# Four second-layer weight blocks converted early and kept in DRAM, and the whole-array block of the scores put first

## The chip, the cores and the metric

The kernel runs on one core of one Trainium2 chip. The metric is the device time of one execution in microseconds (us), the median of the runs shown; lower is better. The engines are TensorE (PE in the profile), VectorE (DVE), ScalarE (ACT), GpSimd (POOL) and SyncE (SP), which issues most DMAs. Each engine works through its own instructions in a fixed order.

## The reference

Three layers follow each other on 4 batches of 448 rows and 768 columns: attention with a sigmoid in place of a softmax, a gated feed-forward (keys, values, receptance), and a Fourier mixing with a second feed-forward.

```python
def _attn_ref(q, k, v):                       # 4 x 12 heads x 448 x 64
    scores = scale * np.matmul(q, k.transpose(0, 1, 3, 2)) - np.log(S)
    attn = 1.0 / (1.0 + np.exp(-scores))
    return np.matmul(attn, v)
def _moe_ref(x, mu_k, mu_r, w_k, w_v, w_r):   # w_k 768 x 1024, w_v 1024 x 768
    x_prev = np.concatenate([zeros, x[:, :-1, :]], axis=1)
    xk = mu_k * x + (1.0 - mu_k) * x_prev
    xr = mu_r * x + (1.0 - mu_r) * x_prev
    k = np.maximum(xk @ w_k, 0.0)
    v = k * k @ w_v
    r = 1.0 / (1.0 + np.exp(-(xr @ w_r)))
    return r * v
def _moe2_ref(x, w_ch1, w_ch2):               # w_ch1 768 x 3072, w_ch2 3072 x 768
    X = np.fft.fft(np.fft.fft(x, axis=1), axis=2)
    u = x + np.real(X)
    un = (u - mean(u)) / np.sqrt(var(u) + 1e-06)
    return u + np.maximum(un @ w_ch1, 0.0) @ w_ch2
```

The weights come as 64-bit floats.

## The kernel before

The program is recorded in an order that a small planner (the class Order, L110) works out: generators such as `attention`, `keys`, `values`, `convert` and `network` yield the time at which they can go on, by costs written into the class, and what they issue is appended to the engines. So a changed cost, wait or task moves instructions of all engines, and at run time each engine keeps to the order that came out.

Products of full precision are made of three matmuls of 448 columns each: every operand is split into a high and a low part (names ending in h and l), and high x high, high x low and low x high are added in PSUM. The stages, in order of time:

**Attention** (0 to about 250 us). The 24 pairs of heads (6 to a batch) go through `scores` and `attnv` (L383, L414). A pair's scores are seven blocks: six of 64 rows, 0 to 5, two of which run side by side in the two halves of the array, and one of 128 rows, block 6 (FULL), that takes the whole array. Their PSUM banks come from `ps2` (five, for the six small blocks) and `ps1` (three, for block 6, the attention output `av` and the tiles `k` of the keys). A sigmoid on ScalarE takes each block out of PSUM (`sg`). Pairs 0 to 5 use plain fp32; from pair 6 on (WHOLE) each block is three split matmuls. Pairs 6 and 7 start with block 6, the later ones end with it (L402). After each pair `join` copies the output out and mixes it with the shifted rows. Between pairs the matmuls of `keys` fill in, as many as the planner puts into PACE (L31) per pair.

**Receptance** (to about 371 us). Meanwhile `load_split` (L256) converts w_v: from the two 32-bit halves of a 64-bit float, bit operations on VectorE and a square on ScalarE make the 32-bit weight, whose low part gets cut off where it is tiny. One block of 128 x 768 is one two-operand and three three-operand instructions of VectorE.

**Values and spectra** (to about 540 us). `values` (L689) multiplies by w_v, VectorE multiplies with the receptance (tiles `rv`, two buffers) into `x2`; per batch `folds`, `spectrum`, `mixed` and `centre` follow on VectorE, ScalarE and TensorE, between the matmuls of the next batch. k tiles are loaded by `load_k2` as their buffers come free.

**The last network**. For batches 0 and 1, `network` (L1133) takes the 12 weight groups one after the other: `ffn1` (w1, tiles `h`), then `ffn2` (w2, tiles `f`, added to `acc` by VectorE, which frees the PSUM bank). Groups 0 and 1 were converted during attention (EARLY, L321) and are loaded. Groups 2 to 11 are converted by `convert` (L976) beside it: load of the 64-bit block, square and bit operations, store into DRAM (`w_d`), high part by ScalarE, low part by GpSimd. `prepare_rows` (L1073) multiplies the rows of batches 2 and 3 by `rsb`. From about 896 us on, batches 2 and 3 go through a scheme of seven products for w1 (`pair1`) and through `ffn2` with the weights from `w_d`. Every second `pair1` begins with a matmul of one column.

Of the kernel before, what the change touches and what calls it, by code (L numbers as in the profile page):

```python
# [12 lines left out]
F32 = mybir.dt.float32  # L13
F32R = mybir.dt.float32r
U32 = mybir.dt.uint32
# [6 lines left out]
D = H * DH  # L22
# [7 lines left out]
TOK = B * S  # L30
PACE = 10.8  # L31
EVERY = (11.6, 9.4)
# [4 lines left out]
PERM = np.concatenate([SL, D - SL, D // 2 - SL, D // 2 + SL, LL, L2])  # L37


TINY = float((2.0**-15 * 1.0625) ** 2)  # L40
# [204 lines left out]
def build(tc, ap):  # L245
# [10 lines left out]
    def load_split(pl, parts, gap=0.0, raws=1, lane=0, eng=None, vector=False, every=0.0):  # L256
# [11 lines left out]
        for i, (wait, src, hi, lo, key) in enumerate(parts):  # L268
# [7 lines left out]
            if callable(hi):  # L276
                hi, lo, after = hi()
            n = o.size(hi)
            if ahead and raws > 1:
                nxt = load(*ahead)  # L280
            if ap["wide"]:
                top, low = raw[:, :, 1], raw[:, :, 0]
                if not vector:
                    w = pl.tile([128, n], F32, tag=f"wst{lane}", name="_".join(map(str, key)), bufs=1)
                bits = pl.tile([128, n], U32, tag=f"wbits{lane}", name="_".join(map(str, (*key, "bits"))), bufs=1)
                if vector:
                    yield o.ts(bits, top, 3, 0x3FFFFFF8, ALU.logical_shift_left, ALU.bitwise_and) - 0.1
                    yield o.stt(bits, top, 0xC0000000, bits, ALU.bitwise_and, ALU.bitwise_or) - 0.1
                    yield o.stt(bits, low, 29, bits, ALU.logical_shift_right, ALU.bitwise_or) - 0.1
                    yield o.tt(V, top.bitcast(F32), top.bitcast(F32), top.bitcast(F32), ALU.mult) - 0.1  # L290
                    w = bits.bitcast(F32)
                    yield o.stt(w, top.bitcast(F32), TINY, w, ALU.is_ge, ALU.mult) - 0.1
                    if ahead and raws == 1:
                        nxt = load(*ahead)
                else:
                    o.act(w, top.bitcast(F32), AF.Square)
                    yield o.ts(bits, top, 3, 0x3FFFFFF8, ALU.logical_shift_left, ALU.bitwise_and) + gap
                    yield o.stt(bits, top, 0xC0000000, bits, ALU.bitwise_and, ALU.bitwise_or) + gap
                    yield o.stt(bits, low, 29, bits, ALU.logical_shift_right, ALU.bitwise_or) + gap
                    if ahead and raws == 1:  # L300
                        nxt = load(*ahead)
                    yield o.stt(w, w, TINY, bits.bitcast(F32), ALU.is_ge, ALU.mult)
            else:
                w = raw
            if vector:
                V.tensor_copy(hi, w)
                o.spend(V, 0.07 + n * 0.00104)
            else:
                yield o.act(hi, w)
# [73 lines left out]
    def scores(i):  # L383
# [16 lines left out]
        else:  # L400
            halves = [(2 * c, 2 * c + 1) for c in range(3)]
            for ns in [(FULL,), *halves] if i < WHOLE + 2 else [*halves, (FULL,)]:  # L402
                ps = {n: room(n) for n in ns}
                for t, (a, b) in enumerate(((0, 0), (0, 1), (1, 0))):
                    for n in ns:
                        c, j = places[n]
                        cost = None if j is None else 0.107
                        o.mm(ps[n][:, 0:S], k[a][rows(j), c], q[b][rows(j)], t == 0, t == 2, cost)
                for n in ns:
                    weigh(i, n, ps[n])  # L410
                yield from o.others()
# [17 lines left out]
    def join(i, ps):  # L429
# [3 lines left out]
        b, p = pairs[i]  # L433
        o.dma(x_d[b][p], x)
        if b > 1:
            yield from o.issued(("key", b - 2))
# [166 lines left out]

    wv_parts = [((), ap["w_v"][:, t], wvh[:, t], wvl[:, t], ("wv", t)) for t in range(NF)]
    NK = 12
    k2_t, un_t, r_t, rs_t = {}, {}, {}, {}
# [42 lines left out]
    o.run(("r_d", B - 1, KD - 1))  # L649
    o.run(("wv", NF - 1))  # L650
    s_r.close()
# [37 lines left out]
    def values():  # L689
        for b in range(B):  # L690
            o.spawn(new_x2(b))
            for e in range(KD):
                while len(o.feed) > 6:
# [243 lines left out]
    w_t = {}  # L937

    def load_early(nm, g, pl):

# [7 lines left out]

    load_early("w1", 0, wq)
    o.spawn(values())  # L950
# [25 lines left out]
    def convert():  # L976
# [19 lines left out]
        for n, (nm, g, i) in enumerate(seq):  # L996
# [12 lines left out]
            w = raw  # L1009
            if ap["wide"]:  # L1010
                top, low = raw[:, :, 1], raw[:, :, 0]
                w = wst.tile([128, D], F32, tag="wst", name=f"{nm}_{g}_{i}", bufs=2)
                bits = wst.tile([128, D], U32, tag="bits", name=f"{nm}_{g}_{i}_bits", bufs=1)
# [332 lines left out]
```

## Time and profile before

| | us |
|---|---|
| three runs | 1231.38, 1226.49, 1226.11 |
| median | 1226.49 |
| profiled execution, its own time | 1231.31 |
| its span, first to last instruction | 1229.5 |
| TensorE busy | 1216.5 (99%) |
| VectorE busy | 907.4 (74%) |
| ScalarE busy | 479.1 (39%) |
| GpSimd busy | 135.3 (11%) |

The busy time of an engine is the time in which at least one of its instructions ran. Matmuls are pipelined: records of neighbours overlap, so the time from one start to the next tells more than a duration. The waits tell whom an engine stood still for. A stretch of time can be asked for each engine's busy time and count of instructions; an instruction that only reaches into the stretch is counted too. All parts of the text that use the word spacing mean the time from one matmul's start to the next one's.

### The profile page before, as it was taken

Reading aid. Unit: us, or ns where it says so; the run is one execution under the profiler, and the core shown is the slowest. Engines: PE = TensorE matmul, PEld = TensorE weight load, DVE = VectorE, ACT = ScalarE, POOL = GpSimd, SP = SyncE. Lnnn points to the kernel's source line nnn. Section 1 sums busy time; section 2 is a strip of 40 time slices with the busy share of each in tenths; the row PEclk is TensorE's granted clock in tenths of the full one; section 3 lists DMA queues with packets and bytes.
Section 4 is the critical chain, followed back from the end, with each engine's and each line's share of the span. In section 5 each row is a group of like instructions: output and inputs, shape, how many; then the busy total and the mean of one; then the engine's idle time right before and its main releaser. Section 6 shows DMA issues by size and latency. Waiting matters only on the chain. (4 is left out here: it accounts for less than half of the span.)

```text
span 1229.5 us, 16416 instructions
## 1 busy us (share of the span) xinstructions
PE 1216.5 (99%) x6142; PEld 1050.5 (85%) x6142; DVE 907.4 (74%) x1425; ACT 479.1 (39%) x864; POOL 135.3 (11%) x97
## 2 busy tenths in 40 slices
PE   8999999999999999999989999999999999999998
PEld 3467766789999998999979999999999999999998
DVE  5776887656853669797999999897566776776654
ACT  5867767766530122142333333332132332322220
POOL 0000000000000000000232232222021111121110
PEclk9999999999999999999999999999999999999999
DMA  6656669666948446396555555555842112121102
GB/s 219 223 169 229 213 239 339 237 243 231 320 158 259 169 165 218 113 316 227 184 202 212 184 200 203 201 186 188 314 141 78 52 54 75 52 66 63 52 1 90
DMA packets 77296, 217.82 MB, mean 177 GB/s; under 512 B 9312, under 2 KB 31776, under 8 KB 76576
## 3 DMA queue, kind: packets, MB, share of 16 engines
q1 hardware_dynamic: 76544, 214.37, 50.3%
q0 software_dynamic: 672, 2.40, 0.6%
q8 instruction: 48, 0.79, 0.3%
q14 instruction: 32, 0.26, 0.1%
HBM read 143.84 MB, written 72.90 MB: 176 GB/s over the span
## 5 line engine op out<-in xcount | busy, mean ns | idle before, releaser
L215 DVE TENSOR_TENSOR acc<-acc,f 128x448 f32<-128x448 f32 x258 | 156.6, 616 | 66.4 <-PE f L180 63.8
L180 PE MATMUL f<-h,w2h 128*128 128x448 f32 x576 | 165.6, 368 | 3.6 <-DVE acc L215 3.6
L180 PE MATMUL f<-un,w1h 128*128 128x448 f32 x576 | 166.2, 368 | 0.0
L180 PE MATMUL f<-h,v2h 128*128 128x448 f32 x576 | 163.6, 365 | 0.0
L180 PEld LDWEIGHTS f<-h,w2h 128*128 128x128 f32 x576 | 107.8, 188 | 14.9 <-DVE acc L215 4.8
L234 ACT ACTIVATE sg<-sc,bias_s 128x448 f32<-128x448 f32 x168 | 95.0, 651 | 60.7 <-PE sc L180 60.7
L180 PEld LDWEIGHTS f<-un,w1h 128*128 128x128 f32 x576 | 108.2, 188 | 10.4 <-issue 0.4
L180 PEld LDWEIGHTS f<-h,v2h 128*128 128x128 f32 x576 | 108.2, 188 | 8.5
L180 PE MATMUL v<-k,wvh 128*128 128x448 f32 x384 | 113.4, 370 | 0.8 <-DMA k<-k_d 0.7
L180 PE MATMUL f<-un,w1l 128*128 128x448 f32 x288 | 105.9, 368 | 0.0
L180 PE MATMUL f<-h,w2l 128*128 128x448 f32 x288 | 105.9, 368 | 0.0
L180 PE MATMUL f<-h,v2l 128*128 128x448 f32 x288 | 105.2, 365 | 0.0
L223 DVE SCALAR_TENSOR_TENSOR w_bits<-w_raw,w_bits 128x768 uint32<-128x768 uint32 x80 | 99.9, 1248 | 1.0
L180 PE MATMUL av<-sg,v 128*64 128x448 f32 (+1 forms) x336 | 81.1, 549 | 0.0
L180 PEld LDWEIGHTS v<-k,wvh 128*128 128x128 f32 x384 | 71.6, 188 | 8.1 <-DMA k<-k_d 2.4
L215 POOL TENSOR_TENSOR v2l<-v,v2h 128x768 fp32r<-128x768 f32 x24 | 46.8, 1970 | 275.0 <-ACT v2h L232 275.0
L215 POOL TENSOR_TENSOR w1l<-w,w1h 128x768 fp32r<-128x768 f32 x20 | 41.2, 2062 | 300.6 <-ACT w1h L232 295.5
L180 PE MATMUL v<-k,wvl 128*128 128x448 f32 x192 | 70.8, 369 | 0.0
L180 PE MATMUL k<-xkh,wkh 128*128 128x448 f32 x192 | 70.7, 368 | 0.0
L180 PE MATMUL k<-xkl,wkh 128*128 128x448 f32 x192 | 70.4, 367 | 0.0
L180 PE MATMUL k<-xkh,wkl 128*128 128x448 f32 x192 | 70.3, 366 | 0.0
L180 PEld LDWEIGHTS av<-sg,v 128*64 128x64 f32 (+1 forms) x336 | 27.9, 144 | 42.5 <-issue 35.9
(175 smaller groups left out, 2356.7 us busy)
## 6 DMA issues: line engine op xcount, KB each, us to landing
w_raw<-in_w SPq DMA_DIRECT2D x40, 768.0 KB, 4.5
w_d<-w SPq DMA_DIRECT2D x40, 384.0 KB, 2.6
k_d<-kp SPq DMA_DIRECT2D x32, 448.0 KB, 2.8
k<-k_d SPq DMA_DIRECT2D x32, 448.0 KB, 6.3
a<-w_d SPq DMA_DIRECT2D x24, 384.0 KB, 3.5
v<-w_d SPq DMA_DIRECT2D x24, 384.0 KB, 3.0
k<-in_k SPq DMA_DIRECT2D x24, 256.0 KB, 5.5
v<-in_v SPq DMA_DIRECT2D x24, 256.0 KB, 3.0
```

The lines of the kernel that those rows point to most:

```text
L180: self.nc.tensor.matmul(out, lhs, rhs, start=start, stop=stop, skip_group_check=skip)
L215: eng.tensor_tensor(out, a, c, op=op)
L223: self.nc.vector.scalar_tensor_tensor(out, a, scalar, c, op0=op0, op1=op1)
L234: self.nc.scalar.activation(out, a, fn, **kw)
```

## The change

Four edits go together.

- AHEAD names groups 2 and 3 of w2, two blocks each. `load_split`, which converts w_v in receptance, gets the two blocks of group 2 at its end and stores them into `w_d`; a new task `ahead` converts those of group 3, in four half blocks, at the beginning of the values, and only then loads w1 of group 0. `convert` loads the four blocks as 32-bit floats from `w_d` and does no bit work on them.
- In `load_split` the square on ScalarE now writes over the raw block, after the second bit operation and not ahead of them, and the separate tile for the weight is gone.
- `scores` starts with block 6 for all pairs from 6 on; `join` waits until the next pair's scores are recorded before it mixes; PACE is 10.6 for 10.8.
- `values` waits until a batch's `x2` tile is taken.

```diff
-PACE = 10.8
+PACE = 10.6
...
+AHEAD = tuple(("w2", g) for g in range(2, 4))
+SOON = 2
...
-                    o.act(w, top.bitcast(F32), AF.Square)
-                    yield o.ts(bits, top, 3, 0x3FFFFFF8, ALU.logical_shift_left, ALU.bitwise_and) + gap
-                    yield o.stt(bits, top, 0xC0000000, bits, ALU.bitwise_and, ALU.bitwise_or) + gap
-                    yield o.stt(bits, low, 29, bits, ALU.logical_shift_right, ALU.bitwise_or) + gap
+                    o.ts(bits, top, 3, 0x3FFFFFF8, ALU.logical_shift_left, ALU.bitwise_and)
+                    yield o.stt(bits, top, 0xC0000000, bits, ALU.bitwise_and, ALU.bitwise_or)
+                    t = o.act(top.bitcast(F32), top.bitcast(F32), AF.Square)
+                    o.stt(bits, low, 29, bits, ALU.logical_shift_right, ALU.bitwise_or)
+                    yield t
+                    yield o.stt(w, top.bitcast(F32), TINY, w, ALU.is_ge, ALU.mult)
...
-                    yield o.stt(w, w, TINY, bits.bitcast(F32), ALU.is_ge, ALU.mult)
...
+            if hi is None:
+                o.at[key] = o.dma(lo, w) + 2.0
+                yield max(o.now, begun + every)
+                continue
...
-            for ns in [(FULL,), *halves] if i < WHOLE + 2 else [*halves, (FULL,)]:
+            for ns in [(FULL,), *halves]:
...
+        if i + 1 < len(pairs):
+            yield from o.issued(("pair", i + 1))
...
+    soon = [(nm, g, i) for nm, g in AHEAD for i in range(2)]
+    if ap["wide"]:
+        wv_parts += [((), ap[nm][2 * g + i], None, w_d[nm][2 * g + i], ("ahead", nm, g, i)) for nm, g, i in soon[:SOON]]
...
-    o.run(("wv", NF - 1))
+    o.run(wv_parts[-1][-1])
...
+            while b not in x2_t:
+                yield o.now + 0.1
...
+    def ahead():
+        n = D // 2
+        seq = [(*k, c) for k in soon[SOON if ap["wide"] else 0 :] for c in range(2)]
...
+            raw = wq.tile([128, n, 2], U32, tag="w1h", name=f"{nm}_{g}_{i}_{c}_raw", bufs=2)
...
+                bits = wq.tile([128, n], U32, tag="w1l", name=f"{nm}_{g}_{i}_{c}_bits", bufs=2)
+                w = bits.bitcast(F32)
...
+            o.at["ahead", nm, g, i, c] = o.dma(w_d[nm][2 * g + i][:, n * c : n * c + n], w) + 2.0
+        load_early("w1", 0, wq)
...
-    load_early("w1", 0, wq)
+    o.spawn(ahead())
...
-            if not ap["wide"]:
-                raw = wst.tile([128, D], F32, tag="wst", name=f"{nm}_{g}_{i}", bufs=2)
-                return raw, o.dma(raw, ap[nm][2 * g + i])
+            if (nm, g) in AHEAD or not ap["wide"]:
+                raw = wst.tile([128, D], F32, tag="wst", name=f"{nm}_{g}_{i}", bufs=3)
+                return raw, o.dma(raw, w_d[nm][2 * g + i] if (nm, g) in AHEAD else ap[nm][2 * g + i])
...
-            o.dma(w_d[nm][2 * g + i], w)
+            if (nm, g) not in AHEAD:
+                o.dma(w_d[nm][2 * g + i], w)
...
-            if ap["wide"]:
+            if ap["wide"] and (nm, g) not in AHEAD:
```

The planner then records many instructions in another order. Three places of it follow; a name such as sc_6_1833 is block 6 of the scores with the number of its tile, av the attention output, k a tile of the keys, qh and kl the split operands.

TensorE, around block 6 of pair 16, before:

```order
L180 MATMUL sc_4_1820<-qh_1596,kl_1600 128x448
L180 MATMUL sc_5_1821<-qh_1596,kl_1600 128x448
L180 MATMUL sc_6_1833<-qh_1596,kh_1599 128x448
L180 MATMUL sc_6_1833<-ql_1597,kh_1599 128x448
L180 MATMUL sc_6_1833<-qh_1596,kl_1600 128x448
L180 MATMUL k_4_1761<-xkl_716,wkh 128x448
```

and after, for the same pair:

```order
L183 MATMUL av_1745<-sg_5_1688,v_1528 64x448
L183 MATMUL sc_6_1766<-qh_1577,kh_1574 128x448
L183 MATMUL sc_6_1766<-ql_1578,kh_1574 128x448
L183 MATMUL sc_6_1766<-qh_1577,kl_1575 128x448
L183 MATMUL sc_0_1777<-qh_1577,kh_1574 128x448
L183 MATMUL sc_1_1778<-qh_1577,kh_1574 128x448
```

Block 6 moved from the end of a pair's scores, ahead of the keys, to their beginning, behind the attention output.

VectorE at the beginning of the values, before (wvl is the low part of the last block of w_v, x_0 the values of batch 0, rv the receptance, evod the folds):

```order
L215 TENSOR_TENSOR wvl<-wv_3784,wvh 128x768
L667 MEMSET one 128x128
L215 TENSOR_TENSOR x_0_3922<-v_0_3920,rv_0_3513 128x448
L215 TENSOR_TENSOR x_0_3922<-v_1_3946,rv_1_3518 128x448
L215 TENSOR_TENSOR evod_3981<-x_0_3922 128x448 x2
```

and after:

```order
L218 TENSOR_TENSOR wvl<-wv_bits,wvh 128x768
L230 TENSOR_SCALAR ahead_w_2_0_bits<-ahead_w_2_0_raw 128x768
L226 SCALAR_TENSOR_TENSOR ahead_w_2_0_bits<-ahead_w_2_0_raw,ahead_w_2_0_bits 128x768 x3
L230 TENSOR_SCALAR ahead_w_2_1_bits<-ahead_w_2_1_raw 128x768
L226 SCALAR_TENSOR_TENSOR ahead_w_2_1_bits<-ahead_w_2_1_raw,ahead_w_2_1_bits 128x768 x3
L680 MEMSET one 128x128
L218 TENSOR_TENSOR x_0_3924<-v_0_3925,rv_0_3501 128x448
L218 TENSOR_TENSOR x_0_3924<-v_1_3950,rv_1_3510 128x448
L230 TENSOR_SCALAR w_3_0_0_bits<-w_3_0_0_raw 128x384
L226 SCALAR_TENSOR_TENSOR w_3_0_0_bits<-w_3_0_0_raw,w_3_0_0_bits 128x384
L218 TENSOR_TENSOR evod_3990<-x_0_3924 128x448 x2
```

The conversion of group 2 stands behind that of w_v, that of group 3 between the first values and their folds.

VectorE in the last network, between the last addition of a group of `ffn2` (f_1_1_5, group 1, batch 1) and the first of the next (f_2_0_0, group 2, batch 0), before (w_3_1 is a block of w1, w_3_0 here the first of w2 of group 3, h the hidden layer, rsb the factors of the rows):

```order
L215 TENSOR_TENSOR acc_5716<-acc_5716,f_1_1_5_6110 128x448
L227 TENSOR_SCALAR w_3_1_bits<-w_3_1_raw 128x768
L215 TENSOR_TENSOR acc_6039<-acc_6039,rsb_5908 128x448
L223 SCALAR_TENSOR_TENSOR w_3_1_bits<-w_3_1_raw,w_3_1_bits 128x768 x2
L223 SCALAR_TENSOR_TENSOR h_1_0_6153<-f_2_1_0_6118,h_1_0_6153 128x448
L223 SCALAR_TENSOR_TENSOR w_3_1_6127<-w_3_1_6127,w_3_1_bits 128x768
L227 TENSOR_SCALAR w_3_0_bits<-w_3_0_raw 128x768
L223 SCALAR_TENSOR_TENSOR w_3_0_bits<-w_3_0_raw,w_3_0_bits 128x768
L215 TENSOR_TENSOR acc_6039<-acc_6039,rsb_6037 128x448
L215 TENSOR_TENSOR acc_5505<-acc_5505,f_2_0_0_6186 128x448
```

and after:

```order
L218 TENSOR_TENSOR acc_5673<-acc_5673,f_1_1_5_6152 128x448
L226 SCALAR_TENSOR_TENSOR w_3_1_6125<-w_3_1_6125,w_3_1_bits 128x768
L218 TENSOR_TENSOR acc_6063<-acc_6063,rsb_6061 128x448
L226 SCALAR_TENSOR_TENSOR h_1_0_6194<-f_2_1_0_6161,h_1_0_6194 128x448
L226 SCALAR_TENSOR_TENSOR h_1_1_6219<-f_2_1_1_6192,h_1_1_6219 128x448
L218 TENSOR_TENSOR acc_5559<-acc_5559,f_2_0_0_6217 128x448
```

Of the nine rows between the two additions four are left.

## Rows read from the trace of the kernel before

**Rows 1.** The page: its head and TensorE's busy time.

```profile
span 1229.5 us, 16416 instructions
...
PE 1216.5 (99%) x6142; PEld 1050.5 (85%) x6142; DVE 907.4 (74%) x1425; ACT 479.1 (39%) x864; POOL 135.3 (11%) x97
```

**Rows 2.** Waits of TensorE: engine line waited for: us in total, times, longest.

```profile
PE f L180 <- DVE acc L215: 3.6, 2, 2.0
PE v L180 <- DMA k<-k_d: 0.7, 2, 0.5
```

**Rows 3.** Stretches: from:to, length, busy (count) of PE, PEld, DVE, ACT, POOL; clock, DMA.

```profile
586.00:615.00 29.00, 29.00 (x145) 26.89 (x144) 27.60 (x37) 9.44 (x14) 8.54 (x5) 1.00 0.56 198
618.00:639.00 21.00, 21.00 (x105) 19.48 (x105) 20.77 (x26) 7.70 (x12) 5.68 (x3) 1.00 0.50 178
645.00:895.00 250.00, 250.00 (x1211) 227.14 (x1211) 218.59 (x279) 77.63 (x118) 61.35 (x31) 1.00 0.59 212
897.00:943.00 46.00, 46.00 (x229) 42.66 (x228) 33.19 (x54) 15.06 (x28) 9.80 (x5) 1.00 0.31 104
```

**Rows 4.** Timeline of TensorE at its two waits: start, us, instruction [idle before].

```profile
615.39 0.36 PE L180 MATMUL f<-h,w2l 128*128 128x448 f32 x1
617.73 0.67 PE L180 MATMUL f<-h,w2h 128*128 128x448 f32 x2 [1.97 <-DVE acc L215]
...
639.52 0.36 PE L180 MATMUL f<-h,w2l 128*128 128x448 f32 x1
641.48 0.68 PE L180 MATMUL f<-h,w2h 128*128 128x448 f32 x2 [1.60 <-DVE acc L215]
```

**Rows 5.** Stretches: the scores of pairs 6, 7 and 11.

```profile
49.11:52.48 3.37, 3.30 (x22) 2.20 (x22) 1.49 (x2) 2.46 (x5) 0.00 (x0) 1.00 0.37 132
56.26:59.76 3.50, 3.30 (x22) 2.22 (x22) 3.50 (x6) 3.10 (x6) 0.00 (x0) 1.00 0.67 214
101.07:104.19 3.12, 3.12 (x23) 2.39 (x22) 0.98 (x2) 2.21 (x5) 0.00 (x0) 1.00 0.94 334
```

**Rows 6.** Timeline of TensorE: last 64-row blocks of pairs 6 and 11; first key matmuls.

```profile
51.24 0.90 PE L180 MATMUL sc<-qh,kh 64*128 64x448 f32 x2
...
59.76 0.47 PE L180 MATMUL k<-xkh,wkh 128*128 128x448 f32 x1
60.07 0.36 PE L180 MATMUL k<-xkl,wkh 128*128 128x448 f32 x1
...
102.41 0.73 PE L180 MATMUL sc<-qh,kh 64*128 64x448 f32 x2
```

**Rows 7.** Stretches: 25 key matmuls behind pair 11 and behind pair 12.

```profile
104.19:109.25 5.06, 5.06 (x26) 4.70 (x25) 1.82 (x3) 5.03 (x11) 0.10 (x1) 1.00 0.95 289
115.63:120.80 5.17, 5.17 (x26) 4.69 (x25) 3.23 (x6) 5.13 (x11) 0.45 (x1) 1.00 0.87 277
```

**Rows 8.** Timeline of VectorE in the last network, at TensorE's two waits.

```profile
607.37 2.22 DVE L227 TENSOR_SCALAR w_bits<-w_raw 128x768 uint32<-128x768 uint32 x1
...
612.44 0.95 DVE L223 SCALAR_TENSOR_TENSOR w<-w,w_bits 128x768 f32<-128x768 f32 x1
...
614.90 2.25 DVE L215 TENSOR_TENSOR acc<-acc,rsb 128x448 f32<-128x448 f32 x1
617.07 0.61 DVE L215 TENSOR_TENSOR acc<-acc,f 128x448 f32<-128x448 f32 x1
...
640.81 0.61 DVE L215 TENSOR_TENSOR acc<-acc,f 128x448 f32<-128x448 f32 x1
```

**Rows 9.** Timeline of VectorE at the beginning of the values.

```profile
375.00 0.62 DVE L215 TENSOR_TENSOR x<-v,rv 128x448 f32<-128x448 f32 x1 [13.15 <-PE v L180]
...
390.21 1.19 DVE L215 TENSOR_TENSOR x<-v,rv 128x448 f32<-128x448 f32 x2 [8.52 <-DMA rv<-r_d]
```

**Rows 10.** Timeline of GpSimd beside rows 8.

```profile
607.33 1.84 POOL L215 TENSOR_TENSOR w1l<-w,w1h 128x768 fp32r<-128x768 f32 x1 [5.56 <-ACT w1h L232]
614.35 2.31 POOL L215 TENSOR_TENSOR w1l<-w,w1h 128x768 fp32r<-128x768 f32 x1 [5.17 <-ACT w1h L232]
```

More of the change, by code (lines that the diff above doesn't have):

```diff
@@ L277, in load_split @@
                 hi, lo, after = hi()
-            n = o.size(hi)
+            n = o.size(src)
             if ahead and raws > 1:
@@ L282, in load_split @@
                 top, low = raw[:, :, 1], raw[:, :, 0]
-                if not vector:
-                    w = pl.tile([128, n], F32, tag=f"wst{lane}", name="_".join(map(str, key)), bufs=1)
-                bits = pl.tile([128, n], U32, tag=f"wbits{lane}", name="_".join(map(str, (*key, "bits"))), bufs=1)
+                bits = pl.tile(
+                    [128, n], U32, tag=f"wbits{lane}", name="_".join(map(str, (*key, "bits"))), bufs=1 if vector else 2
+                )
+                w = bits.bitcast(F32)
                 if vector:
@@ L290, in load_split @@
                     yield o.tt(V, top.bitcast(F32), top.bitcast(F32), top.bitcast(F32), ALU.mult) - 0.1
-                    w = bits.bitcast(F32)
                     yield o.stt(w, top.bitcast(F32), TINY, w, ALU.is_ge, ALU.mult) - 0.1
@@ L937, in build, with load @@
     w_t = {}
+    def ahead():
+        n = D // 2
+        seq = [(*k, c) for k in soon[SOON if ap["wide"] else 0 :] for c in range(2)]
+        def load(nm, g, i, c):
+            src = ap[nm][2 * g + i, :, n * c : n * c + n]
+            if not ap["wide"]:
+                raw = wq.tile([128, n], F32, tag="w1l", name=f"{nm}_{g}_{i}_{c}", bufs=2)
+                return raw, o.dma(raw, src)
+            raw = wq.tile([128, n, 2], U32, tag="w1h", name=f"{nm}_{g}_{i}_{c}_raw", bufs=2)
+            return raw, o.dma(raw, src.bitcast(U32).rearrange("p (n t) -> p n t", t=2))
+        nxt = load(*seq[0])
+        for k, (nm, g, i, c) in enumerate(seq):
+            raw, t = nxt
+            yield t
+            nxt = load(*seq[k + 1]) if k + 1 < len(seq) else None
+            w = raw
+            if ap["wide"]:
+                top, low = raw[:, :, 1], raw[:, :, 0]
+                bits = wq.tile([128, n], U32, tag="w1l", name=f"{nm}_{g}_{i}_{c}_bits", bufs=2)
+                w = bits.bitcast(F32)
+                o.ts(bits, top, 3, 0x3FFFFFF8, ALU.logical_shift_left, ALU.bitwise_and)
+                yield o.stt(bits, top, 0xC0000000, bits, ALU.bitwise_and, ALU.bitwise_or)
+                t = o.act(top.bitcast(F32), top.bitcast(F32), AF.Square)
+                o.stt(bits, low, 29, bits, ALU.logical_shift_right, ALU.bitwise_or)
+                yield t
+                yield o.stt(w, top.bitcast(F32), TINY, w, ALU.is_ge, ALU.mult)
+            o.at["ahead", nm, g, i, c] = o.dma(w_d[nm][2 * g + i][:, n * c : n * c + n], w) + 2.0
+        load_early("w1", 0, wq)
     def load_early(nm, g, pl):
@@ L1009, in convert @@
             w = raw
-            if ap["wide"]:
+            if ap["wide"] and (nm, g) not in AHEAD:
                 top, low = raw[:, :, 1], raw[:, :, 0]
-                w = wst.tile([128, D], F32, tag="wst", name=f"{nm}_{g}_{i}", bufs=2)
+                w = wst.tile([128, D], F32, tag="wst", name=f"{nm}_{g}_{i}", bufs=3)
                 bits = wst.tile([128, D], U32, tag="bits", name=f"{nm}_{g}_{i}_bits", bufs=1)
```

## The prediction

> **What bounds the kernel now.** I read the page first: TensorE (PE) is busy 1216.5 us of a span of 1229.5 [rows 1]. So nothing is won by a faster engine beside it; a change pays only where it ends a wait of TensorE or shortens what TensorE itself does. Its waits come next [rows 2]: beside that for the first load, which the change leaves alone, 3.6 us in two waits for additions on VectorE (DVE) in the last network and 0.7 us for loads of the keys in the values. But a busy TensorE is not one at its best, so I then counted matmuls per stretch [rows 3]. All of these are 448 columns wide, at the same granted clock (1.00, the level of 2.4 GHz), and about two records of each count only reach into the stretch. From 645 to 895 us, 250 us hold some 1209 matmuls, one per 206.8 ns; from 897 to 943 us, 46 us hold 227, one per 202.6 ns; from 586 to 615 and from 618 to 639 us it is 203 to 204 ns. So there are two spacings, 2% apart, for the same work. The first wait (615 us) lies between two stretches of the short one; the second (639 us) ends it, and the long one lasts to 895 us [rows 3, 4].
>
> **The sum is made against the profiled execution**, 1231.31 us (the span and 1.8 us around it). The three runs are 1231.38, 1226.49 and 1226.11; the median is 4.8 us below the profiled execution. 0.5% of the median, about what a measurement can tell from no change, is 6.1 us.
>
> **Part 1, the scores with the whole-array block first.** Pairs 6 and 7 already run in the new order, pairs 8 to 23 in the old one, so the trace holds both prices [rows 5]. A pair's scores take 3.37 and 3.50 us with the whole-array block first (49.11 and 56.26 us), 3.12 us with it last (101.07 us, one of 16 alike). What follows differs too: behind 64-row blocks the first matmul of the keys takes 0.31 us, from 59.76 to 60.07 us [rows 6], instead of 0.20. The extra is one more switch of the array between 128 and 64 rows, and a longer wait of the last 64-row block for a PSUM buffer (0.90 us for the two matmuls at 51.24 us, 0.73 at 102.41 us [rows 6]): the sigmoid that frees it stands behind that of the whole block and the copy of the attention output. Per pair 3.37 + 0.11 - 3.12 = 0.36 us. TensorE has no slack here, so 16 pairs cost 5.8 us. Lower bound: without idle time the new order is busy 3.30 us [rows 5], 0.29 a pair, 4.6 us; upper bound, from pair 7, 0.49 a pair, 7.8 us. I take pair 6, behind whose whole block the sigmoids and the copy stand as they now do for all. Something comes back: the 25 key matmuls between two pairs take 5.06 or 5.17 us [rows 7], the two spacings again, and about half of the pairs had the long one. If the new entry always gives the short one, that is 7 x 0.1 = 0.7 us; I take 0.6. Part 1: **+5.2 us**, bounds +3.9 and +7.8. The pace, 10.6 for 10.8, only changes how many key matmuls stand between two pairs (24 for 25), not their number: nothing.
>
> **Part 2, the conversions that move.** Four blocks of w2 (groups 2 and 3) are converted, two in receptance, two in the values. Each is four instructions on VectorE, none over 0.95 us where undisturbed (612.44 us [rows 8]), so under 3.8 us, and a square on ScalarE. In the trace VectorE does nothing for 13.15 us before the first value (375.00 us) and again for 8.52 us before 390.21 us, where it waits for an r load [rows 9], and TensorE waits for nothing there. The first two blocks, 7.6 us, fit into the first gap; the second two, as four half blocks, into the second and the time around it. If that cover were gone, each block would delay the folds behind it by up to 3.8 us. The queue of SyncE is the other place: the stores of the new blocks wait there for VectorE, and the k and r loads of the values stand behind them. In exchange the four loads of w1 of group 0 move behind the k loads of the second batch, for which TensorE waited 0.7 us. I take 0, bounds -0.7 (that wait gone) and +3.8 (one block's work in the way of the first spectrum).
>
> **Part 3, what the last network gets.** There these four blocks are now loaded from DRAM with no bit work; their split (ScalarE, GpSimd) stays. Both waits of TensorE are VectorE coming late with an addition that frees a PSUM bank. Start to start the first costs 617.73 - 615.39 - 0.20 = 2.14 us, the second 641.48 - 639.52 - 0.20 = 1.76 us [rows 4], and some 0.3 us go in the refill behind them: 4.2 us. How late was VectorE? The addition at 617.07 us was due at 610.7, six matmuls into its group; between the previous group's last addition (until 607.4 us) and it VectorE ran ten instructions, 9.7 us [rows 8]. The new order has four there: one of the conversion, a multiplication and two of the hidden layer. At 0.95 and three times 0.61 that is 2.8 us, or 4.4 if the multiplication meets a GpSimd instruction again as at 614.90 us (2.25 us [rows 8], beside 614.35 us [rows 10]). Either is far under 9.7; the first wait has no cause left. Before the addition at 640.81 us the new order has two three-operand conversion instructions fewer, about 1.9 us, and none of the lateness inherited from 617 us: more than the 1.76 us of the wait. What is late next are the multiplications of the third and fourth batch, which TensorE does not need soon. I take **-4.2 us**, bounds 0 and -4.2.
>
> **Part 4, the spacing.** If TensorE does not stall between 586 and 895 us, it should keep the short spacing that it has at 586 us: 1209 x 4.2 ns = **-5.0 us** against the profiled execution. I believe that this is also what parts the profiled execution from the two shorter runs (5.1 us), which then had the short one all along. By the other end the long one holds from 586 us on: 57 us more at 2%, +1.2 us. The Trainium skill ("TensorE: Matmul & The Clock Gate", section "Back-to-back issue gap") gives one spacing for a width and a clock, by its formula 189 ns for 448 columns. The rows show two, both above it, so the trace does not agree; by the page this term would be nil and the sum 1232.3 us.
>
> **The sum.** 1231.3 + 5.2 + 0 - 4.2 - 5.0 = **1227.3 us**: 0.07% above the median before, no change that can be told.
>
> **The rivals.**
> (a) The long spacing holds from 586 to 895 us: 1231.3 + 5.2 - 4.2 + 1.2 = 1233.5 us, slower by 0.57%. The last one-column matmuls of the variance, which stand at 584 us, decide it, or any short wait behind them. For it: the wait at 639 us did this here, and one run of three has the profiled execution's time. Against: behind those matmuls the short one followed. It turns the sign once it holds for more than some 250 us.
> (b) The stalls stay, since GpSimd and not the bit work makes VectorE late. Beside the subtraction at 614.35 us a multiplication took 2.25 us, and beside that at 607.33 us an instruction of the conversion 2.22 us [rows 8, 10]. All subtractions remain. Then 1227.3 + 4.2 = 1231.5 us with the short spacing, 1236.5 with the long one. Against: ten instructions became four. The Trainium skill ("SBUF — State Buffer", section "Who interferes with whom") says that GpSimd and a VectorE instruction with two SBUF inputs exclude each other for the whole instruction. The 2.25 us agree; by that rule the multiplications go on paying, while a conversion that left can no longer collide.
> (c) Pair 6 is no measure for the later ones: with keys ahead of them ScalarE comes to the scores idle, and the last block waits no longer than in the old order. Then 0.36 falls by 0.90 - 0.73 to 0.19 a pair, 3.0 - 0.6 = 2.4 us, and with the k loads' 0.7 us gone 1227.3 - 5.2 + 2.4 - 0.7 = 1223.8 us.
> (d) The change does not hide what it moves: the stores hold the k and r loads behind them in SyncE's queue, the folds of the first batch come late by a block's 3.8 us, and TensorE waits in the first spectrum: 1231.1 us.
>
> **How the numbers follow.** Forecast 0.45, (a) 0.25, (b) 0.13, (c) 0.10, (d) 0.07. Slower by over 0.5% (above 1232.6 us): three quarters of (a), 0.19, half of (b), 0.06, and 0.01 of (d): 0.26. Faster by over 0.5% (below 1220.4 us) needs (c) and more than my rows hold: 0.06. Within: 0.68. The range goes from (c) with 2 us of doubt to (b) with the long spacing, 1221.5 to 1236.5 us; I leave some 0.15 outside.
>
> **What would show it.** Part 1: scores of pairs 8 to 23 at 3.37 us or more and a first key matmul of 0.31 us; wrong, if they stay near 3.12. Part 2: no wait of TensorE for k loads, and none in the first spectrum. Part 3: no wait of TensorE for the additions from 590 to 660 us. Part 4: 227 matmuls in 46 us up to the last product stage; 222 are the long spacing. The forecast is wrong above all if the spacing falls the other way, or if the scores' new order frees something that I have not seen.

## The result and the profile after

| | us |
|---|---|
| six runs of the kernel before | 1225.38 to 1231.38, median 1226.32 |
| six runs of the changed kernel | 1234.09 to 1239.14, median 1235.49 |
| ratio, 95% interval | 1.0065, 1.0042 to 1.0088 |
| profiled execution of the changed kernel, its own time | 1237.11 |

The change makes the kernel slower by some 0.65%, a little over the 0.5% that the prediction took as what can be told from no change; the interval lies clear of 1. The time lies at the upper end of the range (1221.5 to 1236.5 us), 8.2 us above the likeliest forecast of 1227.3 us.

The page of the changed kernel, head and busy times, answers to [rows 1]: 5.8 us more of span, and TensorE 4 us busier with the same 6142 matmuls.

```profile
span 1235.3 us, 16460 instructions
...
PE 1220.5 (99%) x6142; PEld 1048.5 (85%) x6142; DVE 904.0 (73%) x1433; ACT 482.3 (39%) x866; POOL 132.4 (11%) x97
```

Its waits of TensorE, in the columns of [rows 2] (the first load and one of 0.2 us left out). Those for k loads are gone, those for additions fell from 3.6 to 0.4 us, those for yl and un are new, and those for a sigmoid (sg) rose from 0.2 to 0.9 us:

```profile
PE qa L183 <- DVE yl L218: 2.4, 1, 2.4
PE f L183 <- DVE un L218: 1.1, 2, 0.9
PE sc L183 <- ACT sg L237: 0.9, 2, 0.5
PE f L183 <- DVE acc L218: 0.4, 1, 0.4
```

To see where the time went, I asked for the first and last start of three groups of matmuls: the receptance, the first product of the last network, and the product stages of batches 2 and 3. Before:

```profile
L180 PE MATMUL r<-xrh,wrh x144: 362/363/369, 283.0 to 369.3; 128*128 128x448 f32 x144
...
L180 PE MATMUL f<-un,w1h x576: 358/368/712, 522.7 to 873.2; 128*128 128x448 f32 x192
...
L180 PE MATMUL f_X<-B,blk x228: 164/365/451, 895.9 to 1199.8; 128*128 128x448 f32 x108, 128*128 128x1 f32 x6
```

After:

```profile
L183 PE MATMUL r<-xrh,wrh x144: 360/363/369, 290.0 to 376.3; 128*128 128x448 f32 x144
...
L183 PE MATMUL f<-un,w1h x576: 358/368/471, 531.3 to 879.0; 128*128 128x448 f32 x192
...
L183 PE MATMUL f_X<-B,blk x228: 164/365/450, 901.7 to 1205.6; 128*128 128x448 f32 x108, 128*128 128x1 f32 x6
```

From first start to first start: attention with the keys takes 7.0 us more (290.0 for 283.0), receptance and values 1.6 more (241.3 for 239.7), the last network up to the product stages 2.8 less (370.4 for 373.2), the rest the same. That is the 5.8 us between the two profiled executions. The medians are 9.2 us apart: the profiled execution of before, 1231.31 us, is 5.0 us above its median and that of the changed kernel 1.6 us above its own. The trace of before has the long spacing; that its runs near 1226 us have the short one is inferred, since none of them left a trace.

### The profile page after: what moved, and what is told of

Same layout as the page of the kernel before. It is cut to its first block, busy times and chain, and to the rows that moved or that the text cites. A ratio compares the mean times of both kernels' runs of the same rounds, so it can differ in the third digit from the quotient of the medians.

```text
span 1235.3 us, 16460 instructions
## 1 busy us (share of the span) xinstructions
PE 1220.5 (99%) x6142; PEld 1048.5 (85%) x6142; DVE 904.0 (73%) x1433; ACT 482.3 (39%) x866; POOL 132.4 (11%) x97
## 5 line engine op out<-in xcount | busy, mean ns | idle before, releaser
L226 DVE SCALAR_TENSOR_TENSOR w_bits<-w_raw,w_bits 128x768 uint32<-128x768 uint32 (+2 forms) x84 | 99.7, 1187 | 1.4
L218 POOL TENSOR_TENSOR w1l<-w,w1h 128x768 fp32r<-128x768 f32 x20 | 37.7, 1883 | 313.0 <-ACT w1h L235 303.0
```

The lines of the kernel that those rows point to most:

```text
L218: eng.tensor_tensor(out, a, c, op=op)
L226: self.nc.vector.scalar_tensor_tensor(out, a, scalar, c, op0=op0, op1=op1)
```

## Attention: the order of the scores and what follows it

Stretches of the changed kernel, columns as in [rows 3]: scores and keys of one pair, and two stretches of the last network.

```profile
100.64:104.01 3.37, 3.31 (x23) 2.21 (x21) 0.08 (x1) 2.46 (x5) 0.00 (x0) 1.00 0.59 196
104.01:109.07 5.06, 5.06 (x26) 4.62 (x26) 2.04 (x4) 5.03 (x11) 0.10 (x1) 1.00 1.02 297
...
602.00:705.00 103.00, 103.00 (x510) 95.47 (x509) 89.55 (x113) 33.06 (x50) 26.46 (x14) 1.00 0.54 190
...
710.00:895.00 185.00, 185.00 (x897) 168.04 (x896) 156.95 (x205) 56.93 (x88) 44.26 (x22) 1.00 0.60 213
```

The scores take 3.37 us, as pair 6 foretold, where the old order took 3.12 [rows 5]. The 24 keys behind them take 5.06 us: the first 0.31 us, and the other 23 0.2065 us each, the long spacing. In the trace of before 8 of 15 such stretches of keys between two pairs had the short one; in the changed kernel 12 of 15 had the long one. Two runs look at attention.

**e11, one line of the change on the kernel before:**

```diff
-            for ns in [(FULL,), *halves] if i < WHOLE + 2 else [*halves, (FULL,)]:
+            for ns in [(FULL,), *halves]:
```

> The kernel before with one line of the change: the whole-array block first for all pairs from 6 on; pace 10.8 and join as before. Theory A (the order itself costs): 16 pairs at 0.23 to 0.25 us of the scores and 0.11 us of the first key matmul, 5.4 to 5.8 us, with some 0.3 us for pairs that wait for a sigmoid: first receptance matmul near 289 us (283), median near 1232 us. Rival B (join's wait for the next pair and the pace make the loss, not the order): first receptance matmul under 286 us, median under 1229.

Measured: 1233.38 us, ratio 1.0061 (1.0041 to 1.0081). Its first receptance matmul and a pair's scores and 25 keys:

```profile
L180 PE MATMUL r<-xrh,wrh x144: 362/363/369, 288.9 to 375.2; 128*128 128x448 f32 x144
...
102.08:105.45 3.37, 3.31 (x23) 2.21 (x22) 0.43 (x1) 2.46 (x5) 0.00 (x0) 1.00 0.63 219
105.45:110.71 5.26, 5.26 (x26) 4.80 (x26) 2.45 (x4) 5.20 (x11) 0.10 (x1) 1.00 1.00 314
```

The order alone moves the receptance by 5.9 us (288.9 for 283.0), and join's wait and the pace are not needed for it: rival B falls. Not all of the 5.9 us is the order's own price: behind the first of each stretch the key matmuls, 557 of them, start 205.1 ns apart on average here and 204.3 ns before, which is 0.4 us. The rest of the 7.0 us of the whole change, about 1 us, is longer spacing behind attention and two pairs that wait for a sigmoid.

**e1, the whole change without the moved conversions:**

```diff
-AHEAD = tuple(("w2", g) for g in range(2, 4))
+AHEAD = ()
...
-    o.spawn(ahead())
+    load_early("w1", 0, wq)
```

> The changed kernel without the moved conversions: all 24 blocks of the last network's weights are converted there as before; the whole-array block stays first, the new form of the conversion in attention and receptance stays. Theory A (the loss is made in attention, by the order of the scores): a pair's scores 3.34 to 3.37 us, first key matmul 0.31 us, key spacing mostly 206 ns; first receptance matmul near 290 us as after the whole change (283 before), so about 6.9 us over the kernel before, near 1233 us; the two waits near 615 and 640 us of before are there again, seven us later, and no wait of TensorE for yl in the first spectrum. Rival B (the moved conversions make the loss, the scores cost little): first receptance matmul near 284 us and a time within 2 us of the kernel before, 1226 to 1228 us.

Measured: 1232.11 us, ratio 1.0043 (1.0029 to 1.0057). The loss is there without the conversions, so rival B falls. The kernel is even 3.4 us under the changed one (1232.11 against 1235.49): as the change stands, the moved conversions are a loss. Two misses: the waits near 615 and 640 us did not come back (the section on the values, at e5, tells why), and its keys don't keep one spacing. Stretches of 24 keys behind two neighbouring pairs, in the same order of instructions:

```profile
104.44:109.50 5.06, 5.06 (x26) 4.62 (x26) 2.02 (x4) 5.03 (x11) 0.10 (x1) 1.00 0.97 306
116.11:121.08 4.97, 4.97 (x26) 4.62 (x26) 3.41 (x6) 4.91 (x11) 0.10 (x1) 1.00 0.85 264
```

So the new order doesn't set the spacing of the keys. What does stays open.

## The values: a store, a load behind it, and a queue

In the changed kernel TensorE stops 2.4 us in the first spectrum, at qa. VectorE's timeline (start, us, instruction, idle time before):

```profile
417.96 0.62 DVE L218 TENSOR_TENSOR x<-v,rv 128x448 f32<-128x448 f32 x1 [6.42 <-DMA rv<-r_d]
418.50 0.38 DVE L218 TENSOR_TENSOR yl<-yf,yh 128x223 fp32r<-128x223 f32 x1
```

The planner put the first value of batch 1 ahead of yl, and it waits 6.42 us for its rv load. The queue of SyncE at that time (start, time of the group of issues):

```profile
404.79 0.35 SPq L241 DMA_DIRECT2D w_d<-w_bits  x1
...
406.52 0.76 SPq L241 DMA_DIRECT2D w1h<-w_d  x1
410.80 0.32 SPq L241 DMA_DIRECT2D w1l<-w_d  x1
411.21 0.38 SPq L241 DMA_DIRECT2D k<-k_d  x1
411.69 0.38 SPq L241 DMA_DIRECT2D rv<-r_d  x1
```

The store of the last half block is issued at 404.79 us and lands at 410.78 us by the trace. The last w1l load takes the tile that this store reads, so it starts only at 410.80 us, and the k and rv loads stand behind it. The prediction's rival (d) had the stores of the new blocks hold this queue by waiting for VectorE; it is the loads that follow in `ahead` that hold it, by waiting for a store to land.

**e3, the whole change with later w1 loads:**

```diff
             o.at["ahead", nm, g, i, c] = o.dma(...) + 2.0
+        yield from o.need(("x2", 1, 3))
         load_early("w1", 0, wq)
```

> The whole change, but the four loads of w1 of group 0 wait until the fourth value of the second batch is in. In the changed kernel the last of these loads stood in SyncE's queue from 407 to 411 us, for the store of the last converted half block, whose tile it takes, and the rv load that the first value of batch 1 needs stood behind it. Theory A (that queue makes the first spectrum's wait): TensorE's wait of 2.4 us for yl falls under 0.5 us, and the time by 2 to 2.5 us, to 1233 us. Rival B (VectorE's order alone makes it: the first value of batch 1 stands before yl and would be late anyway): a wait of 2 us or more stays and the time is the changed kernel's within 1 us.

Measured: 1233.06 us, ratio 1.0053 (1.0035 to 1.0071), 2.4 us under the changed kernel. The wait for yl is gone from its waits:

```profile
PE f L183 <- DVE un L218: 2.1, 1, 2.1
PE sc L183 <- ACT sg L237: 0.9, 2, 0.5
PE f L183 <- DVE acc L218: 0.4, 1, 0.4
PE v L183 <- DMA k<-k_d: 0.4, 2, 0.2
```

VectorE's order is unchanged there, and it still waits 2.11 us for rv, but TensorE no longer does: theory A. The wait for un is another matter.

**e5, the kernel before with the smallest edit of the change:**

```diff
             o.spawn(new_x2(b))
+            while b not in x2_t:
+                yield o.now + 0.1
```

> The kernel before with one edit of the change, the smallest: values waits until a batch's x2 tile is taken. No row of the prediction had a price for it. In the runs so far that have this edit, with and without the moved conversions, TensorE waits 1.1 us for un and twice some 0.3 us in the first products of the last network; the kernel before never did. In the planner's order this edit alone puts un_0 and un_1 of the second batch ahead of un_2 to un_5 of what TensorE needs first. Theory A (the edit makes these waits): 1307 + 566 + 488 ns gaps and their refills near 525 and 538 us, about 2.1 us, so 1226.2 + 2.1 = 1228.3 us where the spacing is short (1233 where it is long), less up to 1 us if the short k-load waits of the third batch go. Rival B (the new form of the conversion or the later phase makes them): no un wait, 1226.2 us.

Measured: 1225.49 us, ratio 0.9981 (0.9965 to 0.9996). Half right. The wait for un appears in its waits, beside those of before for k:

```profile
PE f L180 <- DVE un L215: 1.1, 2, 0.9
PE f L180 <- POOL w2l L215: 0.8, 1, 0.8
PE v L180 <- DMA k<-k_d: 0.7, 2, 0.5
```

With two shorter stops near 539 us and the refills it costs 2.1 us, start to start. But both waits for additions near 615 and 639 us are gone too, with no block moved, and in sum the kernel is some 1.3 us better off: its lower runs lie from 1224.3 to 1226.2 us, those of before in this comparison from 1225.6 to 1227.6. (Over half of the runs of before lay near 1230 us in the comparison of e5 to e8, a third or fewer in the others. That makes these four ratios smaller, so I also set the two groups of runs against each other.) The order of VectorE shows why TensorE waits for un. The kernel before makes the low part of un_5 of the first batch ahead of the folds (evod) of the fourth; with the edit it comes behind them. VectorE before, then in e5:

```profile
524.51 0.62 DVE L215 TENSOR_TENSOR un<-un 128x448 fp32r<-128x448 f32 x1
525.04 1.15 DVE L215 TENSOR_TENSOR evod<-x 128x448 f32<-128x448 f32 x2
...
524.89 1.15 DVE L215 TENSOR_TENSOR evod<-x 128x448 f32<-128x448 f32 x2
...
526.76 1.69 DVE L215 TENSOR_TENSOR un<-un 128x448 fp32r<-128x448 f32 x3
```

TensorE's first product ends with un_5 and goes on at 527.43 us. (The expectation has un_0 and un_1 of the second batch ahead of un_2 to un_5 of the first; on VectorE they are not.) Of the fourteen programs, the six with the edit, the changed kernel among them, wait for un, and the eight without it do not. The two waits for additions depend on the edit too: with it they are gone even where no block is moved (e1 and e5, which wait 1.8 and 0.8 us further on); without the edit and without moved blocks the first of them is there (before, e11, e12); without the edit and with moved blocks both are gone (e6 to e10).

## The conversions by themselves

**e2, the whole change with the scores as before:**

```diff
-PACE = 10.6
+PACE = 10.8
...
-            for ns in [(FULL,), *halves]:
+            for ns in [(FULL,), *halves] if i < WHOLE + 2 else [*halves, (FULL,)]:
...
-        if i + 1 < len(pairs):
-            yield from o.issued(("pair", i + 1))
```

> The changed kernel with the scores as before (whole-array block last from the third such pair on, pace 10.8, no wait of join): only the conversions move. Theory A: attention ends as before (first receptance matmul near 283 us); TensorE waits 2 to 3 us for yl in the first spectrum and up to 2 us for un in the first products of the last network; no wait of 1.5 us or more near 615 and 640 us. With the short spacing 1226.3 - 4.3 + 2.6 + 2 = 1226.6 us, equal to the kernel before within 2 us. Rival B (conversions are the loss): 1232 us or more. Rival C (the waits come from attention's new phase, the conversions are clean): 1222 us.

Measured: 1228.64 us, ratio 1.0008 (0.9994 to 1.0022): attention ends as before (first receptance matmul at 283.1 us), the yl wait is 2.1 us, the un wait 1.1 us, and no wait near 615 or 640 us. Gain and losses cancel, as theory A said, but the median is 2 us above its figure: behind the yl wait the granted clock was 0.50 for 3.4 us, which costs some 1.6 us more and stood in no term.

**e12, the control: nothing moved, scores as before, no wait for the x2 tile.** The new form of `load_split` is left of the change, and a third buffer (`wst`) for the blocks of `convert`, which the expectation does not name. `AHEAD` is empty as in e1, the scores are as in e2, and

```diff
-            while b not in x2_t:
-                yield o.now + 0.1
```

> The changed kernel without moved conversions, with the scores as before and without the wait for the x2 tile: what is left is the new form of the conversion in attention and receptance. It is the control for what the moved conversions are worth. Theory A (they alone take away the two waits of TensorE near 615 and 640 us): both waits are there, 3.6 us together, and the median is the kernel before's, 1226 us with the short spacing. Rival B (any shift of the planner's order takes them away, as the wait for the x2 tile alone did): no wait of over 1 us there, 1222 to 1224 us.

Measured: 1228.04 us, ratio 1.0009 (0.9993 to 1.0024). Neither theory has it whole: the wait at 615 us is there as in [rows 4]; the one at 640 us shrank to a delay of 0.2 us, by the new form or by the third buffer. TensorE's timeline, and two stretches around it:

```profile
615.25 0.36 PE L183 MATMUL f<-h,w2l 128*128 128x448 f32 x1
617.61 1.11 PE L183 MATMUL f<-h,w2h 128*128 128x448 f32 x2 [2.00 <-DVE acc L218]
```

```profile
612.00:615.00 3.00, 3.00 (x16) 2.78 (x15) 2.93 (x5) 1.69 (x3) 0.77 (x1) 1.00 0.33 112
618.00:620.80 2.80, 2.80 (x9) 2.45 (x9) 2.80 (x5) 0.00 (x0) 0.00 (x0) 0.50 0.10 37
```

Behind this wait the granted clock is 0.50 (the level of 1.2 GHz) and a matmul takes 0.37 us from start to start: over the nine of this stretch 1.5 us more, which no wait shows.

**e7, both repairs on the kernel of e2:**

```diff
-            while b not in x2_t:
-                yield o.now + 0.1
...
+        yield from o.need(("x2", 1, 0))
         load_early("w1", 0, wq)
```

> Moved conversions alone, two in receptance and two in the values as in the change; scores as before; the w1 loads of group 0 wait for the first value of batch 1 and the wait for the x2 tile is left out. Theory A (the two causes add): against the conversions alone (1228.6) the yl wait of 2.1 us and the un waits of 2.1 us are gone, 1224 us; the two half-block conversions in the values cost nothing visible. Rival B (VectorE's order, the first value of batch 1 ahead of yl, costs by itself): a yl wait of 1 us or more stays, 1226 us.

Measured: 1225.19 us (1221.00 to 1227.57), ratio 0.9961 (0.9945 to 0.9978). Of TensorE's waits these are left:

```profile
PE f L183 <- DVE acc L218: 0.4, 1, 0.4
PE v L183 <- DMA k<-k_d: 0.3, 1, 0.3
PE sc L183 <- ACT sg L237: 0.2, 1, 0.2
```

The two causes add, theory A. Its two groups of runs, 1221.0 to 1222.8 and 1225.1 to 1227.6 us, lie some 4.5 us under those of before in the same comparison, and those of the control e12 lie at before's or at most 0.5 us under: the moved blocks are worth about 4 us in a kernel that has the wait. That is the size of the prediction's Part 3, but not its sum: what e12 pays is one wait and the low clock behind it, not two waits.

**e6, all four blocks in receptance** (on e2, and no wait for the x2 tile):

```diff
-SOON = 2
+SOON = 4
```

> Moved conversions alone, but all four blocks are converted in receptance and none in the values; scores as before, no wait for the x2 tile; so no w1 load waits behind a store, and VectorE's order has yl ahead of the first value of batch 1 again. Theory A (moving conversions is worth the two waits at 615 and 640 us, and it costs only through what it does to the queues of the values): no yl wait, no un wait, short waits of 1 us in all near 700 us: 1226.2 - 4.3 + 1.0 = 1222.9 us with the short spacing (1227 if it turns long near 700 us). Rival B (15 us of conversion don't fit into VectorE's 13 us of idle time ahead of the first value): the first values' products come 2 us late, TensorE waits for PSUM banks near 375 to 385 us, 1225 us or more.

Measured: 1226.86 us, ratio 0.9983 (0.9970 to 0.9997). TensorE waits 4.1 us in the values, so the gain is lost, but not for B's reason. The wait, and VectorE there:

```profile
PE v L183 <- DVE x L218: 4.1, 1, 4.1
...
374.68 3.01 DVE L226 SCALAR_TENSOR_TENSOR ahead_w_bits<-ahead_w_raw,ahead_w_bits 128x768 uint32<-128x768 uint32 x3
386.84 0.17 DVE L678 MEMSET one<- 128x128 f32 x1 [9.15 <-DMA w_d<-ahead_w_bits]
388.34 1.15 DVE L218 TENSOR_TENSOR x<-v,rv 128x448 f32<-128x448 f32 x2 [1.33 <-DMA w_d<-ahead_w_bits]
```

VectorE is done with the blocks at 377.7 us; then it waits 9.15 us for a store, since `one` and then x2 take over the memory that the stored blocks lay in. By the trace the last two stores are issued at 372.76 and 377.72 us, beside the loads of the tables, and land at 386.75 and 388.21 us. Here too a store's landing was the price, not the bit work.

**e10, the whole change with both repairs of e7** (the scores as the change has them):

> The whole change with both repairs: w1 of group 0 loaded behind the first value of batch 1, no wait for the x2 tile; the scores as the change has them. Theory A (the terms add): 6.1 us above the same without the scores' new order (1225.2), 1231.3 us, lowest near 1227; no yl wait and no un wait. Rival B (a good part of the scores' loss is the queues and waits behind attention, shifted by it): 1228 us or less.

Measured: 1229.39 us, ratio 1.0024 (1.0011 to 1.0037), 6.1 us under the changed kernel; no wait for yl or un is left. By the medians it is 4.2 us above e7, between what A and B said. But nine of its twelve runs lie in the lower group, 1229.0 to 1229.9 us, and only five of e7's, 1221.0 to 1222.8; group against group it is some 7 us, which is attention's loss in the changed kernel. The two traces, both with the short spacing up to the product stages, say the same. First receptance matmul of e7, then of e10:

```profile
L183 PE MATMUL r<-xrh,wrh x144: 362/363/370, 283.8 to 370.1; 128*128 128x448 f32 x144
...
L183 PE MATMUL r<-xrh,wrh x144: 360/363/369, 289.9 to 376.2; 128*128 128x448 f32 x144
```

These 6.1 us are all but 0.3 of the difference between the two spans (1221.0 and 1227.4 us), although e7's first load came 0.5 us later. So theory A holds, and a median over two groups is a poor measure of a term.

## The spacing

In the changed kernel's last network the short spacing holds up to 705 us: 508 matmuls in 103 us (two of the 510 only reach in), 202.8 ns. A short wait follows, and from 710 us on 895 matmuls take 185 us, 206.7 ns. TensorE at that wait:

```profile
707.38 0.37 PE L183 MATMUL f<-h,w2l 128*128 128x448 f32 x1
708.19 0.68 PE L183 MATMUL f<-h,w2h 128*128 128x448 f32 x2 [0.44 <-DVE acc L218]
```

In e7 and e10 the same wait stands 0.4 us long at the same place of the program, and behind it the short spacing goes on (a stretch of 185 us of e7; 913 matmuls for 895):

```profile
700.00:885.00 185.00, 185.00 (x915) 171.62 (x914) 157.96 (x205) 56.21 (x87) 43.72 (x22) 1.00 0.61 218
```

So the same instructions behind the same wait fall into either spacing.

**e4, the whole change with twelve matmuls of one column**, one ahead of each group's first second-layer product for batch 0:

```diff
+                if one:
+                    self.mm(ps[0][:, 511:512], lhs.bitcast(F32), rhs[:, 0:1].bitcast(F32), True, True, cost=0.2, skip=True)
             self.mm(ps[0][:, 0:S], lhs, rhs, i == 0, i == n - 1)
...
+                    partial(bank2, f"f2_{g}_{b}_{e}"), len(gi), pair, partial(out_done, g, b, e), one=b == 0 and e == 0
```

> The whole change, with a matmul of one column ahead of each group's first second-layer product for batch 0 (12 of them, some 0.08 us each, 1.0 us in all; their result is overwritten by nothing and read by nothing). Theory A (the spacing is a state that such a matmul sets back to the short one): 202 to 203 ns from 708 to 902 us even if a short wait stands at 706 us, instead of 206.6, so 3.7 us less there than in the changed kernel's profiled execution and 1.0 more for the matmuls: 2.7 us less, 1234.4 us for an execution that had the long spacing, up to 1 us more for one that had the short one; the runs lie closer together than the changed kernel's (5 us). Rival B (the spacing is set by something else, such as the DMA traffic): the long spacing is there again and each run costs 1 us more.

Measured: 1236.01 us (1234.12 to 1238.33), ratio 1.0071 (1.0046 to 1.0096). The stretch is short now, 918 records for 895

```profile
710.00:895.00 185.00, 185.00 (x920) 171.59 (x919) 158.50 (x207) 56.94 (x88) 43.47 (x22) 1.00 0.60 215
```

(twelve of them of one column, since each such matmul leaves two records). But the short wait at 708 us was followed by the short spacing even ahead of the next such matmul, so this run alone doesn't show that they set it; and its runs spread over 4.2 us, hardly less than the 5.1 us of the changed kernel, a miss. The price was a miss too: from the start of a one-column matmul to the next start pass 0.14 us, and the matmul behind it takes 0.08 us longer to the next start than others, so one costs 0.22 us and twelve 2.6 us, not 1.0.

**e8, the same twelve on the kernel of e6:**

> As the one with all four blocks in receptance, and the matmul of one column ahead of each group's first second-layer product for batch 0. Theory A (spacing is a state that such a matmul sets back): no execution has the long spacing between 600 and 890 us, so the times lie in one group instead of two 4 to 5 us apart, 1 us above the lower group of the kernel without them: 1224 us, highest under 1227. Rival B: two groups as before, each 1 us higher.

Measured: 1229.99 us (1227.85 to 1231.98), ratio 1.0009 (0.9996 to 1.0022). One group, but wider than expected and 6 us higher: e6 itself lies 4 us above its forecast, with a wait in the values (4.1 us there, 2.4 here), and the twelve matmuls cost 2.6 us where 1.0 had been set down. Since e6's runs lie in one group as well (1225.35 to 1229.13 us), one group here tells little; the trace tells more. Behind its wait at 701 us the spacing is 206.6 ns over 143 matmuls, up to the next one-column matmul at 731 us, and 202.6 ns from there on.

**e9, three of them on the kernel of e7**, in batch 1 of groups 5, 7 and 9 (`one=(g, b, e) in ((5, 1, 2), (7, 1, 2), (9, 1, 2))`):

> The conversions alone with later w1 loads and without the wait for the x2 tile (median 1225.2, its runs in two groups, 1221.0 to 1222.8 and 1225.1 to 1227.6), and three matmuls of one column, in the third second-layer product of batch 1 of groups 5, 7 and 9, the first of them some 5 us behind the last short wait of TensorE (697 us). Theory A (the two groups differ by the spacing from there to the first product stage, 935 matmuls at 4.0 ns, 3.7 us, and one such matmul sets it back): one group, near 1221.0 + 0.3 = 1221.3 us, median 1221 to 1222.5, highest under 1224. Rival B (the groups are made elsewhere, in keys or values): two groups again, median 1224 to 1225.5.

Measured: 1222.18 us, all seven runs between 1221.74 and 1222.99, ratio 0.9960 (0.9943 to 0.9977). In its trace too the long spacing began behind the wait at 696 us (23 matmuls) and ended at the first one-column matmul at 701 us:

```profile
701.40:886.00 184.60, 184.60 (x915) 171.15 (x914) 154.97 (x204) 56.11 (x86) 42.13 (x22) 1.00 0.60 215
```

The upper group of e7 (1225.1 to 1227.6 us), with seven of its twelve runs, is gone. This is the best kernel of the study, 0.4% under the kernel before; the scores keep their old order in it.

## Why the prediction was right or wrong

**Part 1, +5.2 forecast, about +7 measured.** The mechanism and its price were right: 3.37 us and 0.31 us as read from [rows 5, 6], and e11 gives 5.4 us without the spacing, against 5.8 ahead of the deduction. Wrong was the deduction of 0.6 us: it let the new entry choose the short spacing for the keys, and most of them got the long one (205.7 ns on average in the changed kernel, 0.8 us more). Rival (c), 0.19 us a pair, is refuted.

**Part 2, 0 forecast, about +1.6 measured.** The k waits went, as said. The first spectrum's wait was rival (d)'s, with the place right and the holder of the queue wrong. The step that failed is "I take 0": I looked for time on VectorE, and there was enough; I didn't ask when the memory of each stored tile is taken again.

**The edit without a term.** The wait for the x2 tile had no price in the sum. It reorders VectorE's work behind the values and costs 2.1 us of waits for un (there in e5, gone in e7 and e10).

**Part 3, -4.2 forecast, -3.2 measured.** Both waits are gone; two short ones near 706 us cost 1.0 us, start to start. The control e12 has the first of them and e7 has none, so moving the blocks suffices. It is not the only way: e5 and e1, which have the wait for the x2 tile, lost both waits with every block in place. The changed kernel has that edit too, so there the moved blocks were not needed for these 3.2 us. "The first wait has no cause left" was right, that only the conversions were its cause was not. Rival (b) is refuted.

**Part 4, -5.0 forecast, -1.7 measured.** That the two groups of runs of before are the two spacings fits the later traces of kernels with two groups, but no run of before with a time near 1226 us left a trace. That the short one would last was the step that failed: it lasted until a wait of 0.4 us that I hadn't foreseen, 190 us ahead of the end, and 935 matmuls at 4 ns are 3.7 us. This is rival (a), 120 us later than I had put it; since e7 and e10 kept the short one behind the same wait, which of the two came in this execution was luck. The -1.7 is what is left of the network's 2.8 us: some 1.2 of it is in the stretch that Part 4 priced, the rest ahead of it, where the spacing is shorter too.

In sum against the profiled execution: +7.0 for attention, +1.6 for the values, -3.2 + 2.1 - 1.7 = -2.8 for the network. The errors all had one sign. That the range held the time was luck: its upper end was made for rival (b) with the long spacing, which did not come true.

## What to carry to other kernels

Give every edit of a change a term, a one-line wait in a planner too: it can move waits on another engine far behind it. For a load into a tile that a store has just read, ask when the store lands and what is queued behind the load; twice here that made TensorE wait (2.4 and 4.1 us), while the work that was moved did not. Where back-to-back matmuls have two spacings, read both from the trace and don't credit a change with the better one, unless something in the program sets it, as a matmul of one column did here for 0.22 us.

## What the runs showed of the hardware that I had not expected

- The same 128x448 matmuls ran at 202.6 or 206.7 ns at the granted clock 1.00, each for hundreds of matmuls. A wait of 0.44 us ended the short one (the changed kernel, 708 us), one of 1.17 us the long one (e11, 647 us: 206.6 ns before it, 202.65 behind). All 84 product stages that begin with a one-column matmul began short in the fourteen traces; ahead of four of them the spacing was long (before, the changed kernel, e3, e5), and in e8 and e9 such a matmul ended a long stretch as well; the cause isn't known.
- The granted clock fell to 0.50 behind waits of 2.0 us (e12, the row shown), 2.1 us (e2, e3) and 4.1 us (e6), and stayed at 1.00 behind others of 2.0 (before), 2.4 (the changed kernel, e8) and 2.8 us (e4). Where it fell, it was low for 3.4 us and the wait cost about 1.5 us more than its length (worked out for e12), and no row of the waits says so.
